# Attention and gated feed-forward in one kernel: softmax row sums turned and spread by VectorE, maxima over partitions by one transpose, and a new order of the steps

## The chip, the cores and the metric

The kernel runs on one core of one Trainium2 chip. The metric is the device time of one execution in microseconds. Three executions of the kernel before took 829.94, 830.16 and 830.75 us, a median of 830.16 us. The profiled execution, from which every row below is taken, took 830.94 us, and the span from its first to its last instruction is 829.1 us.

## The reference

Eight batches, twelve heads, 448 positions, head width 64. Attention with normalised queries and keys comes first; its output, heads side by side, is the input of a feed-forward layer with a three-tap convolution along the sequence as a gate.

```python
def _attn_ref(q, k, v, g_q, g_k):
    def rmsnorm(x, g):
        rms = np.sqrt(np.mean(x * x, axis=-1, keepdims=True) + 1e-06)
        return x / rms * g
    q_n, k_n = (rmsnorm(q, g_q), rmsnorm(k, g_k))
    scores = scale * np.matmul(q_n, k_n.transpose(0, 1, 3, 2))
    scores = scores - np.max(scores, axis=-1, keepdims=True)
    attn = np.exp(scores)
    attn = attn / (np.sum(attn, axis=-1, keepdims=True) + 1e-09)
    return np.matmul(attn, v)

def _moe_ref(x, w_in, conv_w, w_out):            # x: [8, 448, 768]
    h = np.maximum(x @ w_in, 0.0)                # w_in: [768, 1024]
    for k in range(3):                           # hp: h padded by one row at both ends
        conv_out += conv_w[k][None, None, :] * hp[:, k:k + S, :]
    gate = 1.0 / (1.0 + np.exp(-conv_out))
    return h * gate @ w_out                      # w_out: [1024, 768]
```

## The kernel before

Two heads of one batch make a pair; there are 48 pairs, n = 0 to 47, six to a batch. A pair's 2 x 448 query rows are laid end to end and cut into seven slots of 128. For a slot, TensorE makes the scores (`scores`, L643), VectorE takes their maximum (`soft_max`, L649), ScalarE makes the exponentials and, in the same instruction, their row sum (`soft_exp`, L657), which goes to one column of the tile `rsum` [128, 7]. The exponentials must stand with the keys on the partitions for the product with v. For pairs 0 to 9 TensorE turns them in f32 (`p_transpose`, L687). From pair 10 on, in six or five of the seven slots, they are split into two f16 parts (`p_hi`, `p_lo`) and turned by a DMA transpose on SP's queue (`p_turn`, L679).

The row sums are needed as divisors of the product with v, where the queries run along the free axis and 64 partitions of each head need the same row. So each pair does this: 1e-9 is added (`sum_add`, L710), VectorE takes the reciprocal (`sum_step`, L713), TensorE turns [128, 7] to [7, 128] in PSUM (`sum_transpose`, L716), ScalarE or VectorE copies that to `rT` (`sum_evac`, L99), a DMA stores it in DRAM as `rd` (`sum_store`, L724), and two DMAs read it back, each spreading one head's 448 numbers over 64 partitions of `rB` (`sum_load`, L730, 112 KB each). `x_scale` (L776, L779) multiplies the finished product with v by `rB` on VectorE, and so frees the product's PSUM bank; `x_hi` and `x_lo` split the result into two f16 parts.

A batch's six pairs are the contraction of the first feed-forward product (`in_part`, L849); its PSUM banks go through `in_relu`, `in_conv`, `in_tanh`, `in_gate`, `in_hi` and `in_lo`, and the second product (`out_part`, L918) makes the output, which is copied out by `out_evac` and stored by `out_store` (L932).

The two weight matrices and each batch's v are scaled by a power of two, from the largest absolute value. The maximum over partitions is taken in four steps: a column [128, 1] is turned to a row (`max_turn`, L191), VectorE reduces the row (`max_row`, L194), TensorE multiplies it by ones to spread it over the partitions again (`max_spread`, L199), and VectorE copies it (`all_max`, L204). That is done ten times, for two weights and eight batches.

What sets the order: each step is planned with a due time (`at`, from the tables `PACE` and `SHIFT`), its needs (`needs`), and its cost on each engine that may do it (`options`). A list scheduler then places step after step on the engine where it comes first, weighing readiness against urgency with the numbers in `PH`. It fixes the order on every engine, which engine takes a step that several may take, and the PSUM bank. Every engine then runs its list strictly in that order, and SP's list is the order in which DMAs are issued.

```python
        t = max((end + lat["DMA" if dma else e] for end, lat in ready[step]), default=0.0)
        kind = ("p_" if i else "f_") + PATIENCE.get(step[0], "")
        waiting[e][step] = t + PH.get(kind, 0.0), c, dma
```

Of the kernel before, what the change touches and what calls it, by code (L numbers as in the profile page):

```python
# [19 lines left out]
PH = dict(  # L20
    sw=0.0, f_pl=0.0372, f_ql=0.301, f_lo=0.0904, f_rms=0.0813, f_sq=0.2875, T=17.3632,
    ti=41.2236, si=4.107, so=8.3066, hop=0.89068, beta=0.014927, wi0=-54.4573, wi1=123.1391,
    wo0=27.8337, wo1=190.2785, cw=120.3485, p_evac=0.8292, p_hi=0.745, p_lo=1.5677, p_rms=0.1994,
    p_v=0.1678, p_x=0.3218, p_g=2.1286, p_relu=18.7486, p_cv=1.0141, p_ev=1.0461, sp=0.053009,
    nbulk=4, p_rs=0.042, p_sq=10.2108, p_w=182.8497, v0=27.1115, nd=6, cs=5, ct=3, cm=9, ne=5,
    n2=0, n1=10, q1=10, nf=10, pvs=4, p_sa=5.3829, p_c0=0.4104, p_ca=1.3841, p_ss=3.937,
    p_qh=3.8564, p_ql=3.3133, p_ph=10.4483, p_pl=23.3405, f_ca=0.5582, f_cv=0.0137, f_ev=0.0025,
    f_evac=0.001, f_g=0.001, f_relu=0.0326, f_v=0.1218, f_w=0.0241,
)
PACE = [  # L30
    20.0962, 19.9026, 16.7987, 18.8982, 12.5992, 14.6433, 12.4646, 10.3051, 23.0432, 17.7085,
    25.8722, 15.4055,
]
SHIFT = dict(
    prepare=752.847, load_g=657.535, make_g=976.01, load_cw=330.398, make_cw=2.091, load=33.068,
    convert=493.531, bound=434.297, bound_max=997.493, bound_turn=110.974, bound_row=439.308,
    bound_spread=144.878, scale=264.777, in_factor=855.239, split=253.006, rest=-5.488,
    out_factor=6.856, load_k=514.422, load_q=-22.79, square=152.084, square_sum=53.339,
    rsqrt=129.836, apply_rms=371.449, qk_transpose=946.516, qk_hi=163.782, v_load=526.719,
    v_bound=-7.992, scores=165.021, soft_max=-3.98, soft_exp=71.301, p_transpose=1089.978,  # L40
    p_evac=1.021, sum_add=292.102, sum_step=3.621, sum_transpose=7.451, sum_evac=951.667,
    sum_store=442.223, sum_load=7.241, pv=277.343, x_scale=531.668, x_hi=50.036, x_lo=5.449,
    v_max=-28.59, v_turn=474.043, v_row=421.545, v_spread=561.379, v_scale=1063.291, qk_lo=-6.16,
    q_hi=-16.404, q_lo=231.56, q_turn=97.487, p_hi=281.925, p_lo=-4.849, p_turn=602.22,
    p_low=0.089, v_hi=46.398, v_lo=369.031, moe_scales=639.368, in_part=826.195, in_relu=654.815,
    in_conv=84.909, in_tanh=377.101, in_gate=187.899, in_hi=137.708, in_lo=1.949,
    in_carry=294.262, out_scales=266.089, out_part=548.912, out_evac=315.656, out_store=-0.364,
# [23 lines left out]
def tile_attention_moe(ctx: ExitStack, tc, q, k, v, g_q, g_k, w_in, conv_w, w_out, out):  # L71
# [41 lines left out]
    def move(e, dst, src):  # L113
# [15 lines left out]
        rB=2, x32=1, vacc=2, vsc=4, cwb=3, rd=2, rsum=2, rT=2, mx=10, ph=4, vp=2,  # L129
# [3 lines left out]
    def new(tag, key, shape, dtype, pool=None):  # L133
        ring = rings.setdefault(tag, Ring(BUFS[tag]))
        pool = pool or sb
        t = pool.tile(
            shape, dtype, tag=tag, name=f"{tag}_{key}".replace(" ", "").replace(",", "_").strip("()"),
            bufs=BUFS[tag],
        )
        return ring.put((tag, key), t)  # L140

# [22 lines left out]
    ones = const.tile([1, P], F32, name="ones")  # L164
    phbuf = [const.tile([P, 2, 4, P], F16, name=f"ph{i}") for i in range(BUFS["ph"])]
    cw_in = const.tile([P, 3, NFC], conv_w.dtype, name="cw_in")
    cw = cw_in if conv_w.dtype == F32 else const.tile([P, 3, NFC], F32, name="cw")
# [4 lines left out]
    NGR = 13  # L172
    gring = const.tile([P, NGR, 2, S], F16, name="gring")
# [1439 lines left out]
```

## Time and profile before

| | before |
|---|---|
| median of 3 runs | 830.16 us |
| profiled execution | 830.94 us |
| its span, first to last instruction | 829.1 us |
| TensorE (PE) busy | 795.0 us, 96% |
| VectorE (DVE) busy | 688.6 us, 83% |
| ScalarE (ACT) busy | 687.6 us, 83% |
| GpSimd (POOL) busy | 451.1 us, 54% |
| DMA queue of SP, share of 16 engines | 75.9% |
| granted TensorE clock, mean | 0.996 |

Busy times are unions over an engine's instructions; instructions that overlap count once. TensorE's matmuls are pipelined and their ends modelled, so what a matmul costs is read from the distance between the starts of neighbours, not from its own duration. Of VectorE's instructions each overlaps the one before it by up to a tenth of a microsecond, so sums of single durations lie above the busy time. Since each engine runs its list in order, an instruction that waits holds all behind it on that engine.

### The profile page before, as it was taken

The page shows a single profiled execution, that of the slowest core. Times are in us where ns is not written, and L with a number is a line of the kernel's source. Part 1 is how long each engine was busy: PE and PEld are TensorE (multiplying, and loading weights), DVE is VectorE, ACT ScalarE, POOL GpSimd, SP SyncE. Part 2 cuts the span into 40 slices and gives each one's busy share as a digit, 9 for nine tenths or more (in the row PEclk, how much of TensorE's full clock was granted, in tenths as well). Part 3 has the DMA queues.
Part 4 walks back from the last instruction along what each step waited for, and adds up shares of the span by engine and source line. Part 5 has one row for each costly group of instructions (what it writes and reads, how often), then busy time and mean ns, then how long its engine had stood idle before and what let it go on. Part 6 is the DMA issues. An engine that isn't in the chain of part 4 may idle for free.

```text
span 829.1 us, 17139 instructions
## 1 busy us (share of the span) xinstructions
PE 795.0 (96%) x5650; PEld 434.0 (52%) x5650; DVE 688.6 (83%) x1387; ACT 687.6 (83%) x1613; POOL 451.1 (54%) x569
## 2 busy tenths in 40 slices
PE   3888999999999999999999999999999999999998
PEld 2434555555544555555545555555545565555554
DVE  7989999998799977999799978998799978781430
ACT  4979999998799977998899987998889978892531
POOL 1312123375677756685587667595587666461210
PEclk9998999999999999999999999999999999999999
DMA  9894644179999999878999999879998997564001
GB/s 244 209 203 104 184 133 124 48 128 201 184 182 182 180 190 196 190 148 195 196 177 185 182 195 200 174 163 192 203 175 179 193 180 161 100 120 102 11 21 57
DMA packets 325640, 132.47 MB, mean 160 GB/s; under 512 B 265312, under 2 KB 321968, under 8 KB 325552
## 3 DMA queue, kind: packets, MB, share of 16 engines
q1 hardware_dynamic: 325552, 131.39, 75.9%
q8 instruction: 44, 0.72, 0.4%
q14 instruction: 44, 0.36, 0.2%
HBM read 56.65 MB, written 11.18 MB: 82 GB/s over the span
## 4 chain that ended last, share of the span: by engine, by line
PE 59%; DVE 13%; ACT 13%; DMA 7%; issue 5%; POOL 2%; SPq 1%; ACTq 0%; POOLq 0%; DVEq 0%
PE bank L918 25%; PE bank L849 11%; PE bank L643 8%; PE bank L765 8%; PE bank L687 5%; DMA PT<-ph 3%; ACT ph L99 2%; PE bank L457 2%; DMA rB<-rd 2%; POOL ph L111 1%; DVE st L397 1%; DMA qkf<-in_q_dram 1%; DVE PT L703 1%; ACT sq L386 1%; ACT bank L857 1%
## 5 line engine op out<-in xcount | busy, mean ns | idle before, releaser
L849 PE MATMUL bank<-x,wi 128*128 128x448 f16 x1152 | 231.3, 353 | 0.1
L918 PE MATMUL bank<-wo,gring 128*128 128x384 f16 (+1 forms) x1056 | 200.0, 327 | 0.0
L849 PEld LDWEIGHTS <-wi 128*128 128x128 f16 x1152 | 110.9, 98 | 100.6 <-issue 7.7
L643 PE MATMUL bank<-kT,qT 64*128 64x448 f16 (+3 forms) x1072 | 131.7, 391 | 3.2 <-DVE wo L230 1.5
L918 PEld LDWEIGHTS <-gring 128*128 128x128 f16 (+1 forms) x1056 | 101.7, 99 | 62.7 <-issue 11.0
L765 PE MATMUL bank<-PT,vp 112*64 112x448 f16 x912 | 93.5, 354 | 0.0
L765 PEld LDWEIGHTS <-vp 112*64 112x64 f16 x912 | 48.5, 110 | 42.5 <-issue 11.2
L397 DVE TENSOR_REDUCE st<-sq 112x16 f32<-112x1024 f32 (+1 forms) x50 | 58.2, 1166 | 5.9 <-ACT sq L386 5.9
L111 POOL TENSOR_TENSOR x<-x,x 128x448 f16<-128x448 f32 x35 | 40.6, 1160 | 37.2 <-ACT x L99 20.4
L643 PEld LDWEIGHTS <-qT 64*128 64x128 f16 (+1 forms) x912 | 32.7, 97 | 48.8 <-issue 29.4
L386 ACT ACTIVATE sq<-qkf 112x1024 f32<-112x1024 f32 (+1 forms) x50 | 50.9, 1019 | 5.4 <-DMA qkf<-in_q_dram 4.0
L111 POOL TENSOR_TENSOR sq<-qkf,st 112x512 f32<-112x512 f32 x43 | 45.4, 1065 | 16.5 <-issue 6.8
L457 PE MATMUL bank<-ident,sq 112*128 112x112 f32 x232 | 32.9, 268 | 16.5 <-DVE st L433 10.5
L776 DVE TENSOR_TENSOR x<-bank,rB 128x448 f32<-128x448 f32 x38 | 23.7, 624 | 29.9 <-PE bank L765 14.2
L918 PE MATMUL bank<-wo,wi 128*128 128x384 f16 (+1 forms) x192 | 46.9, 326 | 0.0
L111 POOL TENSOR_TENSOR qkf<-sq,qkf 112x512 f16<-112x512 f32 x34 | 40.7, 1201 | 6.6 <-DMA PT<-ph 2.4
L703 DVE TENSOR_TENSOR PT<-bank,PT 112x512 f16<-112x512 f32 x57 | 39.0, 684 | 2.7 <-ACT PT L99 2.0
L710 POOL TENSOR_SCALAR rsum<-rsum 128x7 f32<-128x7 f32 x43 | 13.5, 315 | 50.4 <-ACT qT L99 10.1
L857 ACT ACTIVATE bank<-bank 128x448 f32<-128x448 f32 x64 | 33.9, 530 | 7.5 <-PE bank L849 6.7
L457 PEld LDWEIGHTS bank<-ident,sq 112*128 112x128 f32 x232 | 25.5, 143 | 26.6 <-issue 15.5
L99 ACT COPY PT<-bank 112x512 f32<-112x512 f32 x64 | 36.7, 581 | 3.0 <-PE bank L687 2.9
L111 DVE TENSOR_TENSOR sq<-qkf,st 112x512 f32<-112x512 f32 x53 | 39.0, 762 | 0.1
(2232 smaller groups left out, 1973.0 us busy)
## 6 DMA issues: line engine op xcount, KB each, us to landing
qkf<-in_k_dram SPq DMA_DIRECT2D x48, 224.0 KB
v<-in_v_dram SPq DMA_DIRECT2D x48, 224.0 KB
rB<-rd SPq DMA_DIRECT2D x96, 112.0 KB
wo<-in_moe_w_in_dram SPq DMA_DIRECT2D x12, 512.0 KB
gring<-in_moe_w_out_dram SPq DMA_DIRECT2D x16, 384.0 KB
qkf<-in_q_dram SPq DMA_DIRECT2D x24, 224.0 KB
qkf<-in_q_dram SPq DMA_DIRECT2D x48, 112.0 KB
PT<-ph SPq DMA_TRANSPOSE x209
```

The costliest lines, as they stand in the source:

```text
L99: (nc.scalar.copy if e == "ACT" else elementwise(e).tensor_copy)(dst, src)
L111: elementwise(e).tensor_tensor(dst, a, b, op=op)
L386: nc.scalar.activation(sq, x, AF.Square)
L397: nc.vector.tensor_reduce(st, sq, axis=AX.X, op=ALU.add)
L457: nc.tensor.transpose(ps[:, t * PB : (t + 1) * PB], x[:, t], ident[:PB, :PB])
L643: nc.tensor.matmul(ps[u][o, :S], lhs, rhs, start=(i == 0), stop=(whole(m) or i == 2),)
L687: nc.tensor.transpose(ps[:PB, kt * P : (kt + 1) * P], e[:, kt * PB : (kt + 1) * PB], ident)
L703: nc.vector.tensor_tensor(turned(n, j, 1), held["t", ("p", n, j)][:PB].rearrange("p (k q) -> p k q", k=NB), turned(n, j, 0), op=ALU.subtract,)
L765: nc.tensor.matmul(ps[HALF[h], :S], lhs, rhs, start=(i == 0 and k == 0), stop=(i == pvs(n)[-1] and k == NB - 1),)
L849: nc.tensor.matmul(ps[:, :S], wi[:, wl, c, fc * P : (fc + 1) * P], old("x", b * NP + c)[:, xl], start=(i == 0), stop=(i == 3 * NP - 1),)
L857: nc.scalar.activation(ps, ps, AF.Relu, scale=2.0 ** -24)
L918: nc.tensor.matmul(ps[p0 : p0 + m, :NO2], g, wo[:, wl, fc, half * NO2 : (half + 1) * NO2], start=(i == 0), stop=(i == 3 * NFC - 1),)
```

## The change

The turn of the row sums no longer passes TensorE and PSUM. `rsum` becomes [128, 32], two constant tiles cleared once, of which seven columns are used; `sum_turn` transposes it on VectorE in blocks of 32 x 32. The result [128, 32] has in block b, row s, the 32 sums of positions 32b to 32b+31 of slot s; the store to DRAM puts the four blocks side by side, so `rd` is [32, 128] and its first seven rows are what they were. For pairs 0 to 9 the two loads stay as they are. From pair 10 on (`sh=10`, `sm=15`) one load brings each head's row of 448 twice, to partitions 0, 32, 64 and 96 of a single constant tile `row`, and `sum_spread` copies the first partition of each 32 to all 32 with a VectorE shuffle, into `rB`. The tile `row` has one buffer, so a load waits for the shuffle of the pair before; `rT` has one buffer instead of two.

The maximum over partitions is now one transpose of the column repeated 128 times, [128, 128], so that every partition receives the whole row, and one VectorE reduction from PSUM. The steps `bound_row`, `bound_spread`, `v_row` and `v_spread` and the tile `ones` are gone. The convolution weights lie in the spare end of `wi32`, so that their load (`load_cw`) comes after the last `rest` of the first weight. The numbers of the scheduler (`PH`, `PACE`, `SHIFT`, some costs) are others, and for the first nine pairs the allowances on readiness have values of their own. The number of slots turned by DMA is the same for every pair.

```diff
-    sw=0.0, f_pl=0.0372, f_ql=0.301, f_lo=0.0904, f_rms=0.0813, f_sq=0.2875, T=17.3632,
+    sh=10, sm=15, sw=0.0, f_pl=0.0375, f_ql=0.2981, f_lo=0.1439, f_rms=0.7618, f_sq=0.4266,
...
-        rB=2, x32=1, vacc=2, vsc=4, cwb=3, rd=2, rsum=2, rT=2, mx=10, ph=4, vp=2,
+        rB=2, x32=1, vacc=2, vsc=4, cwb=3, rd=2, rsum=2, rT=1, row=1, ph=4, vp=2,
...
-    ones = const.tile([1, P], F32, name="ones")
+    sums = [const.tile([P, 32], F32, name=f"rsum{i}") for i in range(BUFS["rsum"])]
+    rows = [const.tile([P, S], F32, name=f"row{i}") for i in range(BUFS["row"])]
...
+    end = wi32[:, DM // P, 2 * S :]
+    cw = end[:, : 3 * NFC].rearrange("p (k c) -> p k c", k=3)
...
     def max_turn(key, col):
         t = bank("t", ("x", key))
-        nc.tensor.transpose(t[:1, :P], col, ident)
-
-    def max_row(key):
-        nc.vector.tensor_reduce(
-            new("mx", key, [1, 1], F32), held["t", ("x", key)][:1, :P], AX.X, ALU.max
-        )
-
-    def max_spread(key):
-        nc.tensor.matmul(
-            held["t", ("x", key)][:, 256:257], ones, old("mx", key), start=True, stop=True
-        )
+        nc.tensor.transpose(t[:, :P], col.to_broadcast([P, P]), ident)
 
     def all_max(dst_pow, key):
-        nc.vector.tensor_copy(dst_pow, held["t", ("x", key)][:, 256:257])
+        nc.vector.tensor_reduce(dst_pow, held["t", ("x", key)][:, :P], AX.X, ALU.max)
...
     def sum_step(n):
-        nc.vector.reciprocal(old("rsum", n), old("rsum", n))
-
-    def sum_transpose(n):
-        nc.tensor.transpose(
-            bank("t", ("r", n))[:NS, :P], old("rsum", n), ident
-        )
-
-    def sum_evac(n):
-        copy(on["sum_evac", n], new("rT", n, [NS, P], F32), held["t", ("r", n)][:NS, :P])
+        x = old("rsum", n)[:, :NS]
+        nc.vector.reciprocal(x, x)
+
+    def sum_turn(n):
+
+        nc.vector.transpose(new("rT", n, [P, 32], F32), old("rsum", n))
 
     def sum_store(n):
-        queue("rd").dma_start(new("rd", n, [NS, P], F32, pD), old("rT", n))
+        d = new("rd", n, [32, P], F32, pD)
+        queue("rd").dma_start(d.rearrange("s (b i) -> b s i", b=4), old("rT", n))
...
     def sum_load(n, h):
+        d = old("rd", n)[:NS].rearrange("t p -> (t p)").rearrange("(h s) -> h s", h=2)
+        if shuffled(n):
+            r = fixed("row", n, rows).rearrange("(x p) s -> x p s", p=32)[:, 0]
+            queue("rb").dma_start(r, d.unsqueeze(1).to_broadcast([2, 2, S]))
+            return
         if h == 0:
             new("rB", n, [P, S], F32)
-        row = old("rd", n).rearrange("t p -> (t p)")[h * S : (h + 1) * S]
-        queue("rb").dma_start(
-            old("rB", n)[HALF[h]], row.unsqueeze(0).to_broadcast([64, S])
-        )
+        queue("rb").dma_start(old("rB", n)[HALF[h]], d[h : h + 1].to_broadcast([64, S]))
+
+    def sum_spread(n):
+        nc.vector.stream_shuffle(new("rB", n, [P, S], F32), old("row", n), [0] * 32)
...
+        elif name == "load_cw":
+            for c in range(NWI):
+                yield "rest", "in", c
```

How the order moves is shown at three places. In the names a number that follows the tile is the pair or the batch; the last number only tells one use of a buffer from the next.

TensorE, around the turn of pair 30's sums: `bank2` takes the second feed-forward product of an earlier batch (`wo32`, `gring`, `wi32` hold its operands). Before:

```order
L918 MATMUL bank2_68<-wo32_85,gring_86 128x384
L918 LDWEIGHTS gring_86
L918 MATMUL bank2_68<-wo32_85,gring_86 128x384
L716 MATMUL bank6_72<-ident_76,rsum_30_6280 7x128
L918 LDWEIGHTS gring_86
L918 MATMUL bank2_68<-wo32_85,gring_86 128x384
```

In the change no such row is left for any of the 48 pairs; of L199's rows (`max_spread`) none is left either, and TensorE's list is otherwise of the same kinds and counts. It changes between groups of scores or of products with v and other work 249 times, where it did so 244 times.

SP, from the store of pair 30's sums to their last load: `PT` tiles are the turned exponentials, `ph` their source, `qT` turned queries, `v` and `qkf` inputs of later pairs. Before:

```order
L724 DMA rd_30_6628<-rT_30_6592 7x128
L932 DMA out_0_dram<-c_('o'_3_2_1_6622 128x384
L499 DMA_TRANSPOSE qT_33_6645<-qkf_33_6082 128x8x112
L679 DMA_TRANSPOSE PT_31_6594<-ph1_79 128x8x128
L730 DMA rB_30_6680<-rd_30_6628 64x448
L537 DMA v_36_6683<-in_v_dram 112x2x256
L361 DMA qkf_36_6699<-in_k_dram 112x2x256
L679 DMA_TRANSPOSE PT_31_6594<-ph2_80 128x8x128
L730 DMA rB_30_6680<-rd_30_6628 64x448
```

and in the change:

```order
L712 DMA rd_30_6539<-rT_30_6490 4x32x32
L669 DMA_TRANSPOSE PT_31_6488<-ph1_78 128x8x128
L669 DMA_TRANSPOSE PT_30_6252<-ph3_80 128x8x128
L726 DMA row0_83<-rd_30_6539 4x1x448
L497 DMA_TRANSPOSE qT_33_6593<-qkf_33_6059 128x8x112
```

One small load stands where two large ones did, and the last of it is issued after two other DMAs instead of after six.

VectorE, from the turn of pair 24's sums (`rsum0`) to the shuffle of them (`rB_24`), in the change; this pair has the least work between the two of all pairs from 10 to 46 (pair 36 as little):

```order
L708 STREAM_TRANSPOSE rT_24_5156<-rsum0_81 128x32
L639 TENSOR_REDUCE sst_(25_3_5160<-bank7_73 128x1
L639 TENSOR_REDUCE sst_(25_4_5173<-bank5_71 128x1
L837 TENSOR_TENSOR vsc_3_3775<-vsc_3_3775,wsc_88 128x1
L840 COPY vsc_2_2323<-vsc_3_3775 64x1
L841 COPY vsc_2_2323<-vsc_2_2323 64x1
L210 TENSOR_REDUCE vsc_4_5039<-bank2_68 128x1
L214 TENSOR_SCALAR vsc_4_5039<-vsc_4_5039 128x1
L217 TENSOR_SCALAR vsc_4_5039<-vsc_4_5039 128x1
L218 TENSOR_SCALAR vsc_4_5039<-vsc_4_5039 128x1
L395 TENSOR_REDUCE st_28_5090<-sq_29_5202 112x16
L639 TENSOR_REDUCE sst_(25_5_5232<-bank1_67 128x1
```

The row behind these is `L733 STREAM_SHUFFLE rB_24_5240<-row0_83 128x448`. Before, neither instruction was in VectorE's list, which went from the reciprocal to `x_scale` with no other step of the sums between, but for the seven pairs whose `rT` it copied.

## Rows read from the trace of the kernel before

**Rows 1.** Page, busy time (share of the span) by engine, with numbers of instructions.

```profile
PE 795.0 (96%) x5650; PEld 434.0 (52%) x5650; DVE 688.6 (83%) x1387; ACT 687.6 (83%) x1613; POOL 451.1 (54%) x569
```

**Rows 2.** Windows: stretch, length, each engine's busy us (instructions), clock, DMA share, GB/s.

```profile
core 0: us, PE busy (x) PEld busy (x) DVE busy (x) ACT busy (x) POOL busy (x), PEclk, DMA share, GB/s
0.00:156.00 156.00, 132.03 (x758) 71.89 (x759) 145.91 (x345) 137.16 (x333) 39.68 (x75) 0.98 0.64 163
156.00:728.00 572.00, 565.34 (x4229) 307.09 (x4228) 508.79 (x985) 506.55 (x1189) 388.13 (x470) 1.00 0.89 176
728.00:829.10 101.10, 97.61 (x666) 54.99 (x664) 33.95 (x59) 43.89 (x93) 23.28 (x25) 1.00 0.26 62
...
416.00:468.00 52.00, 50.98 (x410) 26.67 (x409) 51.19 (x92) 50.71 (x118) 39.91 (x46) 1.00 0.95 183
520.00:572.00 52.00, 51.74 (x372) 28.66 (x371) 49.80 (x96) 48.30 (x113) 35.67 (x47) 1.00 0.82 170
624.00:676.00 52.00, 51.37 (x438) 28.32 (x437) 49.10 (x92) 47.83 (x114) 38.58 (x45) 1.00 0.93 184
```

**Rows 3.** Timeline of PE around one L716: start, duration, instruction.

```profile
505.32 0.73 PE L849 MATMUL bank<-x,wi 128*128 128x448 f16 x3
505.89 0.27 PE L716 MATMUL bank<-ident,rsum 128*7 128x128 f32 x1
506.00 0.33 PE L918 MATMUL bank<-wo,gring 128*128 128x384 f16 x1
```

**Rows 4.** Timeline of PE around one batch's L199.

```profile
306.57 0.49 PE L918 MATMUL bank<-wo,wi 128*128 128x384 f16 x2
306.89 0.33 PE L918 MATMUL bank<-wo 128*128 128x384 f16 x1
307.15 0.38 PE L199 MATMUL bank<-mx,ones 1*128 1x1 f32 x2
307.46 1.31 PE L643 MATMUL bank<-kT,qT 64*128 64x448 f16 x12
```

**Rows 5.** Groups by line and form: busy, mean ns, idle before, releaser.

```profile
L716 PE MATMUL bank<-ident,rsum 128*7 128x128 f32 x48 | 13.2, 275 | 0.1
L99 ACT COPY rT<-bank 7x128 f32<-7x128 f32 x41 | 10.1, 247 | 1.8 <-PE bank L716 1.5
L99 DVE COPY rT<-bank 7x128 f32<-7x128 f32 x7 | 1.9, 269 | 0.0
L713 DVE RECIPROCAL rsum<-rsum 128x7 f32<-128x7 f32 x48 | 9.3, 194 | 3.9 <-POOL rsum L710 3.6
L418 DVE SCALAR_TENSOR_TENSOR st<-st 112x32 f32<-112x32 f32 x43 | 10.0, 232 | 0.3
L99 DVE CAST x<-x 128x448 f16<-128x448 f32 x8 | 3.8, 479 | 0.1
L776 DVE TENSOR_TENSOR x<-bank,rB 128x448 f32<-128x448 f32 x38 | 23.7, 624 | 29.9 <-PE bank L765 14.2 <-DMA rB<-rd 13.3 <-PE bank L918 1.2
L397 DVE TENSOR_REDUCE st<-sq 112x16 f32<-112x1024 f32 x46 | 55.5, 1208 | 3.0 <-ACT sq L386 3.0
L105 DVE TENSOR_SCALAR kT<-bank,G 128x448 f16<-128x448 f32 x22 | 14.8, 674 | 0.0
L99 DVE CAST PT<-bank 112x512 f16<-112x512 f32 x14 | 9.5, 681 | 1.1 <-PE bank L687 1.1
L194 DVE TENSOR_REDUCE mx<-bank 1x1 f32<-1x128 f32 x8 | 2.2, 276 | 4.4 <-PE bank L191 4.4
```

**Rows 6.** Page, DMA queue (packets, MB, share), and issues (count, KB each).

```profile
q1 hardware_dynamic: 325552, 131.39, 75.9%
...
rB<-rd SPq DMA_DIRECT2D x96, 112.0 KB
```

**Rows 7.** Timeline of SP, one pair's store to its second load.

```profile
480.26 0.64 SPq L724 DMA_DIRECT2D rd<-rT  x1
...
482.87 0.54 SPq L730 DMA_DIRECT2D rB<-rd  x1
...
486.46 0.58 SPq L730 DMA_DIRECT2D rB<-rd  x1
```

**Rows 8.** Timeline of DVE: one L649 row and the `x_scale` of that pair.

```profile
488.56 0.61 DVE L649 TENSOR_REDUCE sst_(31_4_6565<-bank 128x1 f32<-128x448 f32 x1
489.81 0.64 DVE L776 TENSOR_TENSOR x<-bank,rB 128x448 f32<-128x448 f32 x1 [0.64 <-issue]
```

**Rows 9.** Chain that ended last, 400 to 420 us: start, duration, what.

```profile
411.25 4.07 DMA rB<-rd
```

**Rows 10.** Waits: engine, line, releaser: us in total, times, longest us.

```profile
DVE x L776 <- DMA rB<-rd: 13.3, 13, 2.0
ACT ph L99 <- DMA PT<-ph: 19.8, 23, 2.3
```

More of the change, by code (lines that the diff above doesn't have):

```diff
@@ L37 @@
[L37 to L42, printed above, removed]
@@ new lines @@
+    load=31.489, convert=814.375, bound=1163.815, bound_max=1185.545, bound_turn=683.508,
+    scale=1588.906, in_factor=1190.579, split=219.334, rest=-3.777, out_factor=13.562,
+    load_k=276.969, load_q=-23.205, square=644.465, square_sum=176.751, rsqrt=204.636,
+    apply_rms=466.723, qk_transpose=49.891, qk_hi=700.581, v_load=1413.524, v_bound=41.813,
+    scores=154.339, soft_max=-4.033, soft_exp=1280.605, p_transpose=1204.209, p_evac=1.285,
+    sum_add=984.669, sum_step=662.828, sum_store=217.691, sum_load=507.067, pv=524.491,
@@ L654, in soft_exp @@
         if j == 0:
-            new("rsum", n, [P, NS], F32)
+            fixed("rsum", n, sums)
         c = slot(n, j)
@@ L809, in plan_attention @@
         at(s + 2.5, sum_step, n)
-        at(s + 3.0, sum_transpose, n)
-        at(s + 3.5, sum_evac, n)
+        at(s + 3.0, sum_turn, n)
         at(s + 4.0, sum_store, n)
-        for h in range(2):
+        for h in range(loads(n)):
             at(s + 6.0, sum_load, n, h)
+        if shuffled(n):
+            at(s + 7.0, sum_spread, n)
         if nd(n):
@@ L1190, in needs @@
             yield "sum_store", n
-            yield "x_scale", n - BUFS["rB"]
+            if shuffled(n):
+                for m in range(n):
+                    yield "sum_spread", m
+            else:
+                yield "x_scale", n - BUFS["rB"]
             if a[1]:
                 yield "sum_load", n, 0
+        elif name == "sum_spread":
+            yield "sum_load", n, 0
+            yield "x_scale", n - BUFS["rB"]
         elif name == "pv":
@@ L1207, in needs @@
             yield "x_lo", n - BUFS["x32"]
-            for h in range(2):
-                yield "sum_load", n, h
+            if shuffled(n):
+                yield "sum_spread", n
+            else:
+                for h in range(2):
+                    yield "sum_load", n, h
         elif name == "x_hi":
@@ L1392, in tile_attention_moe, with patience @@
     waiting = {e: {} for e in ("PE", "DVE", "ACT", "POOL", "SP")}
+    MOE = ("in_", "out_", "moe_")
+    def patience(i, name, *a):
+        kind = ("p_" if i else "f_") + PATIENCE.get(name, "")
+        if a and isinstance(a[0], int) and a[0] < (1 if name.startswith(MOE) else PH["early"]):
+            kind += "_early"
+        return kind
     def enqueue(step):
@@ L1396, in enqueue @@
             t = max((end + lat["DMA" if dma else e] for end, lat in ready[step]), default=0.0)
[L1397 to L1398 removed]
+            waiting[e][step] = t + PH.get(patience(i, *step), 0.0), c, dma
     sys.setrecursionlimit(20000)
@@ L1472, in tile_attention_moe @@
             enqueue(step)
-    SCHED.update(most=most, nd=nd, steps=steps, options=options, needs=needs, takes=takes, give=give, BUFS=BUFS, PATIENCE=PATIENCE,
+    SCHED.update(most=most, nd=nd, steps=steps, options=options, needs=needs, takes=takes, give=give, BUFS=BUFS, PATIENCE=PATIENCE, patience=patience,
                  LAT=LAT, OVER=OVER, ISSUE=ISSUE, shared=shared, BULK=BULK, mode=mode)
```

134 lines of the change are left out of this document (63 added, 71 removed).

## The prediction

> **What bounds the kernel now.** I read the page first, then windows over three stages, then timelines of single instructions. The page says that TensorE is busy 96% of the span, VectorE and ScalarE 83% each [rows 1]. A share over the whole span hides its stages, so the windows come next [rows 2]. In the first 156 us TensorE is busy 132.0 us, so it idles 24 us; VectorE is busy 145.9 of the 156. There TensorE waits for VectorE and ScalarE: the f32 pairs run, and the weights are converted. From 156 to 728 us TensorE is busy 565.3 of 572 us, at a granted clock of 1.00, and idles only 6.7 us. This is the stage that bounds the kernel, and its bound is TensorE's list. In the last 101 us the feed-forward products of the last batches remain, TensorE is busy 97.6 us, and VectorE has little to do. In the middle stage VectorE is busy 508.8 of 572 us and the DMA engines have a share of 0.89, so both stand close behind.
>
> Two things follow. A matmul that is taken out of the middle stage shortens it by the distance between the starts of its neighbours, if the others keep up. And no wait that is cured there can give more than 6.7 us in all.
>
> **The turn of the sums on TensorE goes.** In the timeline a turn of `rsum` starts at 505.89 and the next matmul at 506.00, while the three L849 ahead of it run at their usual distance (505.32 to 505.89) [rows 3]. So a turn takes 0.11 us of TensorE's list. Its own duration of 275 ns [rows 5] is the depth of the pipeline and would overstate it two and a half times. 48 x 0.11 = 5.3 us.
>
> **The spreading of the maxima goes.** The pair of L199 instructions stands from 307.15 to 307.46, 0.31 us [rows 4]; ten of them make 3.1 us. The transpose ahead of them stays and still streams 128 columns; that it now fills 128 output partitions instead of one is counted as nothing, with 10 x 0.11 = 1.1 us as the upper bound if it took twice as long.
>
> Together 8.4 us. Ten of the turns and four of the maxima (both weights, batches 0 and 1) lie in the first stage, 10 x 0.11 + 4 x 0.31 = 2.3 us. TensorE idles there, so only half of it is counted: 7.2 us remain. If all or none of the 2.3 counts, it is 8.4 or 6.1.
>
> **Changes of kind.** In front of L199 the last L918 takes 0.26 us to the next start, where the two before it take 0.16 [rows 4]. TensorE's list has five more changes between scores, products with v and the rest; at 0.10 us each that is 0.5 us more.
>
> **VectorE gets more.** A turn of 128 x 32 is not in this trace. From below it is bounded by the reciprocal of seven columns, 194 ns, from above by 232 ns for a two-input operation on 32 columns [rows 5]; with 0.21, 48 make 10.1 us. A shuffle of 128 x 448 is not in it either. The cheapest row over 448 columns is the cast at 479 ns, the dearest comparable the copy of 512 columns at 681 ns; nearest in columns, type and output is `x_scale`, 624 ns [rows 5]. 38 x 0.62 = 23.7 us, between 18.2 and 25.9. The Trainium skill (VectorE: DVE Perf Modes, The perf-mode tier table) gives the shuffle a price, about 2400 ns for 2048 elements in its one mode; scaled to 448 that is an estimate of 525 ns, and the 38 would be 19.9 us, while the sum of the forecast, where they are covered, stays the same. What VectorE loses: seven copies of `rT` (7 x 0.269 = 1.9), ten reductions of a row (10 x 0.276 = 2.8), and 18 of its 23 evacuations of `kT` go to ScalarE (18 x 0.674 = 12.1); it takes over 13 evacuations of `PT` (13 x 0.681 = 8.9) [rows 5]. Net about +26 us; smaller moves are not priced. Some 23 of them fall in the middle stage, where VectorE would be busy 532 of 572 us, 93%. I cost this at nothing, because TensorE sets the pace and VectorE has 63 us of idle time there [rows 2]. If that cover goes, it costs up to the whole 23.
>
> **ScalarE** loses 41 copies of `rT` (10.1 us [rows 5]) and gains the `kT` evacuations; nothing counted.
>
> **DMA.** 76 of 96 loads of 112 KB go, 8.7 of 131.39 MB [rows 6], or 6.6%; 38 loads of 7 KB and a wider store come. By bytes that would be 0.066 x 0.759 x 829 = 42 us of the engines' time at most. What waits for it now: VectorE 13.3 us at `x_scale` and ScalarE 19.8 us for a free `ph` [rows 10], both behind TensorE's pace. Between 0 and the 6.7 us of TensorE's idle time; I take 0, since the same wait appears again at the shuffle.
>
> **The wait at the shuffle.** VectorE's list is in order, so the shuffle holds all scores' maxima behind it until its row has landed. Before, a store was issued at 480.26, its first load at 482.87, its second at 486.46 [rows 7], and `x_scale` started at 489.81 [rows 8], at most 3.4 us behind the issue; elsewhere the chain has 4.1 us [rows 9]. With one load, issued 2.6 us behind the store, a row lands 6.0 to 6.7 us after the store's issue. In the new order the work between turn and shuffle is least at pair 24: three maxima at 0.61 [rows 8], one reduction at 1.21 [rows 5], one of 0.28 and six small ones of some 0.2, about 4.5 us; VectorE then waits some 2 us. The other pairs have mostly 6 to 9 us by the same pricing. If a dozen pairs wait 1.5 us each, that is 18 us in place of the 13.3 now: VectorE's own idle time, and nothing more is counted.
>
> **The sum.** 830.94 - 7.2 + 0.5 = 824.2 us, against the profiled execution. That one is 0.78 us above the median, so against the median I expect **823.5 us**.
>
> **Rivals.**
> 1. *The first stage gets better too.* It has 24 us of TensorE idle time, and its steps get their own numbers in the scheduler. Against it: VectorE is busy 94% there and receives ten turns more. If a third of the idle time went, 8 us, the time would be 815.5.
> 2. *Nothing is won, since VectorE is the next bound.* In the three fullest windows it is busy 51.2, 49.8 and 49.1 of 52 us [rows 2], and 23 us over 572 add 2.1 to each 52: the first is over-full, the other two full. If TensorE waits 2 us in each of these three, 6 us, 829.5 remain. For it speak these windows; against it, that they can pass work to ScalarE, which has fewer evacuations of sums.
> 3. *Slower: the row comes late at every shuffle.* Place: pairs 10 to 47, the shuffle at the head of VectorE's list, the maxima of the next scores behind it, TensorE behind those. The store now writes 128 pieces of 128 bytes (the tile is [128, 32]) where it wrote seven of 512. The point that decides is a row that takes longer than the 7 us of a typical cover. At 2 us beyond it, 38 x 2 = 76 us of waits would fill the 63 - 23 = 40 us that VectorE has left, and up to 36 would reach TensorE; ScalarE and the order's slack take a part of these, and with half of them the time is 823.5 + 18 = 841; at 1 us beyond, 38 us would just fit. The Trainium skill (DMA: Bandwidth & Descriptors, Specifications) speaks for this rival: it asks for at least 512 bytes a piece and has smaller ones written by read-modify-write. No row of this trace shows the time of such a store by itself; by that rule the store would be slower, and by the 2.6 us of the rows it would not matter.
> 4. *The change does not do what it says* can be left out: in the new order the turns, the loads and the spreading matmuls are gone from the lists.
>
> **How the numbers follow.** About 0.2%, 1.7 us, is what a measurement of this kernel can tell from no change: 828.5 to 831.8. I give the forecast 0.52; its own range is 819 to 828.5, with the 6.1 and 8.4 us of the first two terms, a few microseconds for the idle time that the DMA relief may give, and the same for waits at the shuffle. Rival 1 has 0.21, rival 2 0.13, rival 3 0.14. Faster is the forecast and rival 1, 0.73; same is rival 2, 0.13; slower is rival 3, 0.14. The range runs from 815, which leaves out a part of rival 1, to 832, which leaves out nearly all of rival 3.
>
> **What would show it.** No turn of `rsum` on TensorE; in 156 to 728 us a stretch of the same work shorter by some 6 us at nearly full busy time. The turn at about 0.21 us, the shuffle at about 0.62, VectorE at some 93% of the middle stage. At the shuffle waits of some 20 us in total with row loads as releaser; over 60 us, with TensorE's idle time in the middle stage above 15 us, would mean rival 3. TensorE idle time in the first 156 us well under 24 us means rival 1. The prediction is wrong if TensorE's idle time in the middle grows by the 6 us that its list lost, or if the time falls without that list being the reason.

## The result and the profile after

The changed kernel takes **819.88 us** (median of four executions, 819.17 to 821.95) where the kernel before took 830.45 (four, 829.94 to 831.14). The ratio is 0.9876, with a 95% interval of 0.9857 to 0.9896: 10.3 us faster. The forecast of 823.5 us was 3.6 us too high; the time lies in its range, near its fast end of 819, and the gain is above the 8.4 us that the two terms of its sum allow at most. The profiled execution took 819.89 us, its span is 818.1 us.

The page of the changed kernel, busy time by engine, and the three stages of the windows view (stretch, length, busy us with instructions of PE, PEld, DVE, ACT, POOL, clock, DMA share, GB/s):

```profile
PE 787.5 (96%) x5582; PEld 429.3 (52%) x5582; DVE 704.5 (86%) x1478; ACT 683.4 (84%) x1584; POOL 445.9 (55%) x575
```

```profile
0.00:156.00 156.00, 134.16 (x769) 73.07 (x770) 146.24 (x346) 138.93 (x333) 46.96 (x88) 0.98 0.61 167
156.00:728.00 572.00, 566.85 (x4239) 307.11 (x4237) 530.17 (x1080) 511.97 (x1190) 382.23 (x471) 1.00 0.87 164
728.00:818.10 90.10, 86.47 (x578) 49.10 (x576) 28.14 (x55) 32.54 (x64) 16.72 (x17) 1.00 0.20 53
```

Against [rows 1, 2], TensorE is 7.5 us less busy in total and as full as before in the middle stage: 5.2 us idle of 572, where it was 6.7. VectorE is 21.4 us fuller there, as the turns and shuffles were bound to make it. The groups of the new operations, by form, then the shuffle's and ScalarE's waits:

```profile
L733 DVE STREAM_SHUFFLE rB<-row 128x448 f32<-128x448 f32 x38 | 24.9, 656 | 0.0
L708 DVE STREAM_TRANSPOSE rT<-rsum 128x32 f32<-128x32 f32 x48 | 9.7, 202 | 0.2
L109 DVE CAST PT<-bank 112x512 f16<-112x512 f32 x25 | 17.0, 680 | 0.0
L115 DVE TENSOR_SCALAR kT<-bank,G 128x448 f16<-128x448 f32 x5 | 3.4, 672 | 0.0
```

```profile
DVE rB L733 <- DMA row<-rd: 11.2, 16, 1.6
ACT ph L109 <- DMA PT<-ph: 26.4, 34, 2.6
```

The shuffle waits for its row 16 times, 11.2 us in all, in place of the 13.3 us of `x_scale` before [rows 10]. ScalarE's wait for a free `ph` did not shrink with the large loads, it went from 19.8 to 26.4 us.

Where the time came from is read from the second feed-forward product, whose first instruction closes the first stage. The source view of L918, before and then after (count, duration min/median/max in ns, first and last start in us):

```profile
L918 PE MATMUL bank<-wo,gring x1056: 323/326/350, 177.7 to 824.8; 128*128 128x384 f16 x155, 128*64 128x384 f16 x21
```

```profile
L918 PE MATMUL bank<-wo,gring x1056: 322/326/350, 173.1 to 813.7; 128*128 128x384 f16 x153, 128*64 128x384 f16 x23
```

It starts 4.6 us earlier (177.7 to 173.1) and ends 11.1 us earlier. So some 4.6 us come from ahead of this product, where the forecast had counted 1.2 (half of 2.3), and 6.5 from behind its start, where it had counted 5.5 (7.2 - 1.2 - 0.5).

### The profile page after: what moved, and what is told of

Read it like the earlier page. It is cut to its first block, busy times and chain, and to the rows that moved or that the text cites. A ratio compares the mean times of both kernels' runs of the same rounds, so it can differ in the third digit from the quotient of the medians.

```text
span 818.1 us, 16993 instructions
## 1 busy us (share of the span) xinstructions
PE 787.5 (96%) x5582; PEld 429.3 (52%) x5582; DVE 704.5 (86%) x1478; ACT 683.4 (84%) x1584; POOL 445.9 (55%) x575
## 3 DMA queue, kind: packets, MB, share of 16 engines
q1 hardware_dynamic: 325364, 123.56, 74.4%
## 4 chain that ended last, share of the span: by engine, by line
PE 48%; DVE 13%; ACT 11%; DMA 6%; issue 4%; POOL 2%; SPq 2%; ACTq 0%; POOLq 0%; DVEq 0%
PE bank L918 21%; PE bank L849 11%; PE bank L764 6%; PE bank L633 6%; DMA PT<-ph 4%; PE bank L677 2%; ACT ph L109 2%; SPq L669 1%; PE bank L455 1%; POOL ph L121 1%; DMA rd<-rT 1%; DVE st L395 1%; DMA row<-rd 1%; DVE PT L693 1%; ACT bank L857 1%
## 5 line engine op out<-in xcount | busy, mean ns | idle before, releaser
L918 PE MATMUL bank<-wo,gring 128*128 128x384 f16 (+1 forms) x1056 | 199.5, 327 | 1.0 <-ACT e_(34_4_7306 L647 0.8
L918 PEld LDWEIGHTS <-gring 128*128 128x128 f16 (+1 forms) x1056 | 101.7, 99 | 67.9 <-issue 16.4
L764 PEld LDWEIGHTS <-vp 112*64 112x64 f16 x912 | 50.5, 110 | 42.1 <-issue 15.0
L121 POOL TENSOR_TENSOR sq<-qkf,st 112x512 f32<-112x512 f32 x38 | 39.9, 1056 | 19.1 <-issue 9.6
L121 POOL TENSOR_TENSOR x<-x,x 128x448 f16<-128x448 f32 x33 | 34.2, 1036 | 27.6 <-DVE x L109 12.3
L455 PE MATMUL bank<-ident,sq 112*128 112x112 f32 x232 | 33.0, 268 | 15.8 <-DVE G L974 10.3
L918 PE MATMUL bank<-wo,wi 128*128 128x384 f16 (+1 forms) x192 | 46.9, 326 | 0.0
L121 DVE TENSOR_TENSOR sq<-qkf,st 112x512 f32<-112x512 f32 x58 | 44.8, 791 | 0.1
L121 POOL TENSOR_TENSOR qkf<-sq,qkf 112x512 f16<-112x512 f32 x32 | 37.1, 1160 | 5.6 <-DVE sq L121 4.1
L918 PE MATMUL bank<-wo,carry 128*64 128x384 f16 x192 | 34.0, 328 | 0.5 <-DVE c_(1_6_3169 L879 0.5
L542 DVE TENSOR_REDUCE vacc<-v 112x1 f32<-112x512 f32 x48 | 32.2, 674 | 2.4 <-DMA v<-in_v_dram 1.9
```

The source lines that it names most:

```text
L121: elementwise(e).tensor_tensor(dst, a, b, op=op)
L455: nc.tensor.transpose(ps[:, t * PB : (t + 1) * PB], x[:, t], ident[:PB, :PB])
L542: nc.vector.tensor_reduce(old("vacc", b)[:PB, i : i + 1], old("v", n).rearrange("p h t d -> p (h t d)"), axis=AX.X, op=ALU.max, apply_abso ...
L764: nc.tensor.matmul(ps[HALF[h], :S], lhs, rhs, start=(i == 0 and k == 0), stop=(i == pvs(n)[-1] and k == NB - 1),)
L918: nc.tensor.matmul(ps[p0 : p0 + m, :NO2], g, wo[:, wl, fc, half * NO2 : (half + 1) * NO2], start=(i == 0), stop=(i == 3 * NFC - 1),)
```

## The experiments

Four theories were set against one another. **P**: TensorE's list sets the pace of the middle stage, and each instruction taken off it is won. **O**: the gain comes from the new order. **V**: VectorE sets the pace. **D**: the large loads held up the DMAs. In microseconds below, a ratio is multiplied by 830.45; against the changed kernel means less its 0.9876.

### One part of the change at a time, in the order of before

*The maxima alone.* The reduced row then stands in all partitions, and the spreading matmul is left out:

```diff
-        nc.tensor.transpose(t[:1, :P], col, ident)
+        nc.tensor.transpose(t[:, :P], col.to_broadcast([P, P]), ident)
...
-        nc.vector.tensor_copy(dst_pow, held["t", ("x", key)][:, 256:257])
+        nc.vector.tensor_copy(dst_pow, old("mx", key))
```

> The kernel before with its own order; only the maxima are taken in the new way (one transpose of the repeated column, one reduction; the spreading step issues nothing). Theory P (TensorE's list sets the pace of the middle stage): the 20 spreading matmuls go, 10 x 0.31 us = 3.1 us, of which those of the first 156 us count half: 1.9 to 3.1 us faster than before, 827.3 to 828.6. Theory O (the gain comes from the new order and not from the work taken off TensorE): within 1 us of before. Theory V (VectorE sets the pace): no change, as VectorE keeps its three steps.

Measured: 0.9987 (0.9971 to 1.0004), 1.1 us faster and not clear of nothing.

*The turn alone.* The sums are turned by VectorE at the place of the old turn, the large loads stay:

```diff
-        nc.tensor.transpose(
-            bank("t", ("r", n))[:NS, :P], old("rsum", n), ident
-        )
+        nc.vector.transpose(new("rT", n, [P, 32], F32), old("rsum", n))
...
+        queue("rd").dma_start(d.rearrange("s (b i) -> b s i", b=4), old("rT", n))
```

> The kernel before with its own order; only the row sums are turned by VectorE, at the place where TensorE turned them, and the copy from PSUM is gone; the two large loads stay for all pairs. Theory P: 48 x 0.11 us leave TensorE's list, 38 of them in the middle stage: 4.2 to 5.3 us faster than before, about 825.5. Theory O: within 1.5 us of before. Theory V: slower by some of the 8 us that VectorE gains (48 x 0.21 less 7 x 0.27), 832 to 838.

Measured: 0.9993 (0.9981 to 1.0006). The 48 turns left TensorE's list, and the time did not move. In the middle stage:

```profile
156.00:728.00 572.00, 561.58 (x4185) 302.51 (x4184) 510.28 (x1011) 500.54 (x1155) 381.89 (x470) 1.00 0.92 177
```

TensorE idles 10.4 us where it idled 6.7. What was taken off its list came back as waiting. VectorE, at 510 us, is hardly fuller than before (509), which speaks against V. On SP the store takes longer, a median of 582 ns where it took 320:

```profile
L728 SPq DMA_DIRECT2D rd<-rT x48: 563/582/897, 33.1 to 753.4; - x48
```

*Turn, small load and shuffle together*, the shuffle right ahead of `x_scale`:

```diff
+        if n >= 10:
+            nc.vector.stream_shuffle(old("rB", n), old("rB", n), [0] * 32)
```

> As the run with the turn alone, and from the eleventh pair on one small load in place of two large ones and a VectorE shuffle right ahead of x_scale, in place in the tile of the divisors. Still the order of before. Theory P: VectorE has room for 23.7 us more, so the time stays within 1.5 us of the run with the turn alone, about 825. Theory V: 5 to 20 us slower than the turn alone. If the large loads held the DMA engines up (theory D), 2 to 6 us faster than the turn alone.

Measured: 0.997 (0.9955 to 0.9985), 2.5 us faster; 1.9 us of that by the step from large loads to small ones, although VectorE carries the shuffles. By the intervals of both runs the step lies between 0.3 and 3.5 us.

*All three operations in the order of before.*

```diff
+        nc.tensor.transpose(t[:, :P], col.to_broadcast([P, P]), ident)
...
+        nc.vector.transpose(new("rT", n, [P, 32], F32), old("rsum", n))
...
+            nc.vector.stream_shuffle(old("rB", n), old("rB", n), [0] * 32)
```

> The order, the scheduler's numbers and the engines of the steps stay those of before; all three changes of operations are made in it (maxima by one repeated turn, sums turned by VectorE, one small load and an in-place shuffle right ahead of x_scale from pair 10 on). Singly the maxima gave a ratio of 0.9987 and turn plus shuffle 0.997. Theory A (the operations add up, and are worth some 3 to 4 us in a fixed order; the rest of the 11 us came with the new order): a ratio of 0.9957, 826.9 us, between 825.5 and 828.5, and the first second-stage product no earlier than before by more than 1 us. Theory O (the order is only a carrier; together the operations give most of the gain): 823 us or less. If the parts hinder each other: 828.5 or more.

Measured: 0.9974 (0.9959 to 0.9988), 2.2 us faster. That is no more than the parts would add up to (3.6 us; the difference is within the intervals), and far from 10.3. So in the old order the operations give about a fifth of the gain.

### The scheduler's numbers alone

The changed operations, planned with the numbers of before (`PH`, `PACE`, `SHIFT`), and the operations of before, planned with the new numbers and the separate allowances for the first pairs. A part of the first edit (the second is its reverse):

```diff
 PACE = [
-    19.5944, 19.8948, 16.4648, 19.6082, 13.2431, 14.9147, 11.825, 10.1937, 22.5592, 19.3385,
-    25.6034, 15.2494,
+    20.0962, 19.9026, 16.7987, 18.8982, 12.5992, 14.6433, 12.4646, 10.3051, 23.0432, 17.7085,
+    25.8722, 15.4055,
```

> The operations of the changed kernel, ordered with the scheduler's numbers of before (no values of their own for the first nine pairs). Theory P: the work taken off TensorE counts in any order that keeps it fed: 3 to 8 us faster than before, 822.5 to 827.5, with the first stage up to 156 us as before (the start of the second feed-forward product near 177 us). Theory O: within 2 us of before, or slower.

> The operations of before, ordered with the scheduler's numbers of the change (its due times, allowances, and values of their own for the first nine pairs). Theory P: the gain in the first stage, 4.5 us up to the start of the second feed-forward product, came from these numbers, and the rest of the order is worth nothing: 1 to 4 us faster than before, 826 to 829, with that start near 173 us. Theory O: most of the 10.6 us, 820 to 823.

Measured: 1.0081 (1.0053 to 1.0109) for the new operations with old numbers, 1.0213 (1.0184 to 1.0241) for the old operations with new ones. Both are slower than before, the second against every expectation. Neither half carries the gain, so theory O, taken alone, falls too. The numbers seem to fit only the operations that they were chosen with. The old ones have no shift of the due time for the two new steps, so the first plan is also an untuned one.

### One cost added or taken away, in the order of the change

*No shuffle.* Two large loads stand where the small load and the shuffle stood, 24.9 us of VectorE fewer; `rB` has a third buffer:

```diff
-            queue("rb").dma_start(r, d.unsqueeze(1).to_broadcast([2, 2, S]))
+            for i in range(2):
+                queue("rb").dma_start(old("rB", n)[HALF[i]], d[i : i + 1].to_broadcast([64, S]))
...
-        nc.vector.stream_shuffle(new("rB", n, [P, S], F32), old("row", n), [0] * 32)
```

> The changed kernel with its own order; in place of the one small load and the shuffle, two large loads at the place of the load, for all pairs, with one more buffer for the divisors. Theory P: the shuffle is covered and the large loads were covered, so within 1.5 us of the changed kernel, 818.5 to 821.5. Theory V: VectorE loses 23.7 us, so 3 to 10 us faster than the changed kernel. Theory D: 2 to 6 us slower, 822 to 826, with more waits of ScalarE for DMA transposes.

Measured: 1.0076 (1.0055 to 1.0096), 16.6 us above the changed kernel, where theory D had expected 2 to 6. Middle stage, and ScalarE's wait:

```profile
156.00:728.00 572.00, 555.66 (x4125) 300.35 (x4123) 504.26 (x985) 498.63 (x1155) 375.98 (x462) 1.00 0.90 176
```

```profile
ACT ph L109 <- DMA PT<-ph: 37.3, 43, 2.7
```

VectorE is 26 us emptier there and TensorE idles 16.3 us instead of 5.2. The wait that grew is not one for `rB` but ScalarE's for the transposes of `ph`, DMAs that stand behind the loads in SP's list.

*48 more transposes on TensorE*, 128 x 7 to 7 x 128 like the old turn, into a part of a bank of the second feed-forward product that nobody reads:

```diff
+            nc.tensor.transpose(ps[:NS, NO2:], ident[:, :NS], ident)
```

> The changed kernel with its own order, and 48 extra f32 transposes on TensorE of the size of the old turn of the sums (7 columns of weights, 128 columns streamed), one ahead of each of the first 48 blocks of the second feed-forward product, into unused columns of its bank; nobody waits for them. Theory P: each costs its 0.11 us, 48 x 0.11 = 5.3 us, 825.1. Theory O or V: TensorE has idle time to hide them, under 2 us, below 822.

Measured: 0.9912 (0.9893 to 0.9932), 3.0 us above the changed kernel where their places on the list make 5.3. With both intervals that is 0.7 to 5.3 us, so in this order P holds for a part, perhaps for all.

*Each shuffle twice*, the second over the first:

```diff
+        for _ in range(2):
+            nc.vector.stream_shuffle(rb, old("row", n), [0] * 32)
```

> The changed kernel with its own order, each of the 38 shuffles done twice: 23.7 us more on VectorE. Theory P: VectorE would be busy some 554 of 572 us of the middle stage, so part of the cover is gone; 2 to 8 us slower, 822 to 828, well under the 23.7 us added. Theory V (VectorE already sets the pace): close to the full 23.7 us, 838 to 844.

Measured: 0.9996 (0.9979 to 1.0012), 10.0 us above the changed kernel for 24.9 us of added VectorE work, a little above what P had expected. VectorE's cover is partly used up; 0.4 us is lost for each microsecond added.

### Bytes or issues

To split theory D, two loads were added behind each row load, into a spare place in DRAM that nobody reads, once as large as the old ones and once as small as the row load:

```diff
+            for i in range(2):
+                queue("rb").dma_start(z[HALF[i]], d[i : i + 1].to_broadcast([64, S]))
```

```diff
+            for i in range(2):
+                queue("rb").dma_start(z[:, i], d.unsqueeze(1).to_broadcast([2, 2, S]))
```

> The changed kernel with its order, its small row load and its shuffle as they are; right behind each of the 38 row loads SP issues two more loads of 112 KB of the same source into a spare place in DRAM, which nobody reads. No engine waits for them, so the only thing that returns of the old loads is their share of the DMA engines and of SP's list. The version with two large loads in place of load and shuffle stood 16.5 us above the changed kernel. Theory D (the large loads hold up the transfers behind them, the turned exponentials above all): most of that returns, 830 to 837 us, with ScalarE's wait for the transposes of ph at 33 us or more (26.4 in the changed kernel, 37.3 with the large loads). Theory W (what cost there was x_scale waiting for a late row or the missing shuffle): 820 to 823 us and that wait near 26.

> As the run with spare large loads, but the two spare loads behind each row load are small, 7 KB each like the row load itself. The number of DMAs that SP issues is the same as there, the bytes are not. Theory D-bytes (the time that the packets take on the DMA engines is what holds up the others): no more than 2 us above the changed kernel, 819 to 822. Theory D-issue (each DMA on SP's list costs its place there, 76 of them 0.5 to 0.6 us each): half or more of what the large spare loads cost, 825 or more.

Measured: 1.0378 (1.0346 to 1.0409) with the large spare loads, 41.7 us above the changed kernel; 1.0231 (1.021 to 1.0252) with the small ones, 29.5 us above it. The first is far above the 830 to 837 us expected of theory D: the spare loads come on top of the row loads and the shuffles, which the run with two large loads did without. The larger loads' bytes are worth 12 us; the other 29.5 us come with 76 DMAs of 7 KB that nobody reads. The queue in the page, with the small ones (packets, MB, share of 16 engines), is no busier than the changed kernel's 74.4%, which speaks against the packets:

```profile
q1 hardware_dynamic: 325820, 124.10, 71.2%
```

Of theory D the greater part stands in the form of D-issue, beside the 12 us that go with the bytes. ScalarE's wait for `ph` in the run with small spare loads:

```profile
ACT ph L109 <- DMA PT<-ph: 53.5, 57, 2.6
```

*The store with fewer pieces.* The 25 unused rows of each block of 32 are not stored; that takes four stores of seven pieces:

```diff
-        queue("rd").dma_start(d.rearrange("s (b i) -> b s i", b=4), old("rT", n))
+        for b in range(4):
+            x = old("rT", n)[32 * b : 32 * b + NS]
+            queue("rd").dma_start(d[:NS, 32 * b : 32 * b + 32], x)
```

> The changed kernel, but the store of the turned sums leaves out the 25 unused rows of each block of 32: four stores of 7 pieces of 128 bytes instead of one of 128 such pieces. The 25 rows of rd that nobody reads are not written; the output is the same. If the many small pieces make the row late (rival 3 in small): VectorE waits at the shuffle fall from 11.2 to 6 us or less and the time by 1 to 3 us, 817 to 819. If a store's time does not hang on its pieces, three more DMAs a pair on SP's list only cost: 820 to 823 us, the waits at the shuffle at 11 us or above.

Measured: 1.0137 (1.0113 to 1.016), 21.7 us above the changed kernel, where 0 to 3 had been expected for the three further stores. Waits at the shuffle rose from 11.2 to 33.0 us:

```profile
DVE rB L735 <- DMA row<-rd: 33.0, 30, 2.8
```

So this run says nothing on the time that small pieces take to land. It agrees with a price of a DMA on SP's list, but does not separate that from the later row.

### What SP's list costs

What a DMA takes on SP is a row of the trace. The source views of the store and of the two kinds of load (count, ns min/median/max, first and last start), before:

```profile
L724 SPq DMA_DIRECT2D rd<-rT x48: 282/320/861, 34.6 to 754.1; - x48
L730 SPq DMA_DIRECT2D rB<-rd x96: 450/538/1514, 37.8 to 757.5; - x96
```

after:

```profile
L712 SPq DMA_DIRECT2D rd<-rT x48: 541/574/646, 31.7 to 739.4; - x48
L726 SPq DMA_DIRECT2D row<-rd x38: 532/542/614, 186.6 to 741.5; - x38
L730 SPq DMA_DIRECT2D rB<-rd x20: 450/470/1180, 37.0 to 168.5; - x20
```

and the added or changed ones of the runs with large loads back, with small spare loads, with large spare loads and with four stores:

```profile
L727 SPq DMA_DIRECT2D rB<-rd x76: 457/579/1413, 187.8 to 759.5; - x76
```

```profile
L729 SPq DMA_DIRECT2D spare<-rd x76: 554/564/1060, 189.8 to 774.9; - x76
```

```profile
L729 SPq DMA_DIRECT2D spare<-rd x76: 518/577/1497, 188.5 to 786.8; - x76
```

```profile
L714 SPq DMA_DIRECT2D rd<-rT x192: 269/293/914, 32.2 to 765.8; - x192
```

A load of 7 KB keeps SP as long as one of 112 KB, 0.54 us by both medians. The large loads back are 76 x 0.579 - 38 x 0.542 = 23.4 us more on SP, for 16.6 us of time. The small spare loads are 76 x 0.564 = 42.9, for 29.5. The four stores are 192 x 0.293 - 48 x 0.574 = 28.7, for 21.7. That is 0.71, 0.69 and 0.76 us of time for each microsecond of SP's list. The agreement is weaker than it looks. The first run also carries the larger loads' bytes (some 12 us by the two spare runs) and is rid of the shuffles (some 10 us by the doubled shuffle), two terms that nearly cancel; the third also makes rows late at the shuffle. Only the small spare loads come near to adding nothing else. The large spare loads, 43.9 us of SP and 41.7 of time, stand higher, which fits bytes that come on top.

SP's timeline in the changed kernel at a full place (start, duration, line):

```profile
464.29 0.52 SPq L359 DMA_DIRECT2D qkf<-in_k_dram  x1
464.86 0.46 SPq L535 DMA_DIRECT2D v<-in_v_dram  x1
465.43 2.63 SPq L669 DMA_TRANSPOSE PT<-ph  x2
468.11 0.58 SPq L369 DMA_DIRECT2D qkf<-in_q_dram  x1
468.73 0.57 SPq L712 DMA_DIRECT2D rd<-rT  x1
469.40 2.61 SPq L669 DMA_TRANSPOSE PT<-ph  x2
472.11 0.61 SPq L726 DMA_DIRECT2D row<-rd  x1
472.78 0.40 SPq L932 DMA_DIRECT2D out_dram<-c_('o'_3_0_0_6073  x1
473.28 2.66 SPq L669 DMA_TRANSPOSE PT<-ph  x1
475.98 0.57 SPq L932 DMA_DIRECT2D out_dram<-c_('o'_3_0_1_6150  x1
```

Each issue starts within 0.12 us of the end of the one before. A DMA more in such a stretch moves every transpose of exponentials behind it. Not every stretch is like this one. Added up over the middle stage, SP's DMA instructions take some 446 of 572 us (458 before), and in between SP itself waits, longest for GpSimd's part of `ph`:

```profile
SPq L669 <- POOL ph L121: 56.6, 42, 7.9
```

So SP's list is not full. What an added DMA costs there, as far as the waits show, is that the transposes behind it start later.

The Trainium skill (DMA: Bandwidth & Descriptors, Issuing engines are not separate DMA queues) says that the time a sequencer needs to start a DMA is usually small relative to the DMA itself. For one large load the trace agrees: 0.54 us on SP, and 4.07 us of such a load on the chain [rows 7, 9]. But in this kernel 365 plain DMAs and 247 transposes share one list, and the runs above show that DMAs added to it cost time. What no run separates is SP's own time from anything that the queue behind it does per DMA.

## Why the prediction was right, and which steps of it were not

**The bound.** The forecast's account of TensorE came true. Its busy time fell by 7.5 us, both times at a mean granted clock of 0.996, where the sum had 8.4 - 0.5 = 7.9 for the whole list. Its idle time in the span fell by 3.5 us (34.1 to 30.6), 2.1 of them in the first 156 us, and the middle stage is as full as before (566.9 of 572). That a shorter list is enough is not confirmed. With the same operations in the old order 2.2 us were won, and with the turn alone TensorE's idle time in the middle grew from 6.7 to 10.4 us, toward the sign that the forecast had named for being wrong. The condition "if the others keep up" was assumed and not worked out; it held in the new order and, with the turn alone, not in the old one. In that the forecast had luck: nothing in its sum tells the one order from the other.

The bound was read from 6.7 us of idle time, but an engine with little idle time can still be held by others a little everywhere: in the new order 48 transposes put back cost 3.0 of 5.3 us, a second shuffle 10.0 of 24.9, and added DMAs some 0.7 of each microsecond on SP.

**The turn of the sums, 5.3 us.** By itself, in the old order, it gave 0.6 (between a gain of 1.6 and a loss of 0.5). The step that failed is "a matmul that is taken out of the middle stage shortens it by the distance between the starts of its neighbours, if the others keep up". They did not keep up there. One thing that grew is the store: that of 128 pieces keeps SP 0.582 us in this run where that of seven kept it 0.320, 48 x 0.262 = 12.6 us more on SP's list. The forecast had priced the wider store by when it lands (rival 3) and not by what it takes to issue. That this is what ate the gain is not shown, as no run has the turn without the wider store, and at 0.7 us for each microsecond it would have been 8.8 us, more than the 5.3.

**The maxima, 3.1 us.** By themselves 1.1, with an interval from a gain of 2.4 to none. That the repeated column adds nothing to the transpose is right by its row: L207 at 392.88 is followed by the next matmul at 392.99, 0.11 us.

```profile
392.88 0.27 PE L207 MATMUL bank<-ident,vsc 128*128 128x128 f32 x1
392.99 1.46 PE L918 MATMUL bank<-wo,gring 128*128 128x384 f16 x8
```

**VectorE.** The turn took 202 ns (forecast 210), the shuffle 656 (forecast 620). The Trainium skill (VectorE: DVE Perf Modes, The perf-mode tier table) gives about 2400 ns for 2048 elements; the forecast's estimate of 525 ns from it is not borne out by the 656. The middle stage is at 530.2 us busy, forecast 532. All of VectorE gained 15.9 us and not 26. Of the priced moves, the casts of `PT` went from 14 to 25 and those of `kT` from 22 to 5, about as forecast [rows 5]; the rest of the difference lies in moves that were not priced. The cost of nothing is doubtful: by the doubled shuffle, 24.9 us of further shuffles cost some 10 us in this order. Whether the first ones cost as much, inside the result, no run shows.

**DMA, costed at nothing: the step with the weakest ground.** It was bounded by TensorE's idle time in the middle, 6.7 us, and "I take 0, since the same wait appears again at the shuffle". The bound on a gain held: that idle time fell by 1.5 us. But putting the loads back costs 16.6 us, since idle time can grow by more than it can shrink. The wait that grew with it is not at the shuffle or at `x_scale` but ScalarE's for the DMA transposes. The issues of 0.54 to 0.64 us stood in [rows 7] and were read for when a row lands, not for what they hold up. SP's list had for these DMAs 48 x 0.320 + 96 x 0.538 = 67.0 us before, and has 48 x 0.574 + 38 x 0.542 + 20 x 0.470 = 57.5 now: 9.5 us shorter. At 0.7 us each that would be 6.6 us, about what came behind the first L918. This is only a sum that fits, as TensorE's own account does. Two things speak against a fixed price. ScalarE's wait for `ph`, in which the added DMAs show, is longer in the changed kernel than before (26.4 and 19.8 us). And in the old order the same wait fell from 25.4 us with the turn alone to 13.4 with the small loads, for 1.9 us of time:

```profile
ACT ph L99 <- DMA PT<-ph: 25.4, 27, 2.6
```

```profile
ACT ph L99 <- DMA PT<-ph: 13.4, 17, 2.0
```

**The wait at the shuffle.** 11.2 us in 16 waits, the forecast had 18 in a dozen. Pair 24, whose cover was priced at 4.5 us with a wait of 2, had none; its shuffle started 7.0 us behind the turn, because VectorE had waited for TensorE's turn of a maximum (0.99 us) and for ScalarE's squares (1.85) on the way:

```profile
390.56 0.20 DVE L708 STREAM_TRANSPOSE rT<-rsum 128x32 f32<-128x32 f32 x1
...
393.19 0.29 DVE L210 TENSOR_REDUCE vsc<-bank 128x1 f32<-128x128 f32 x1 [0.99 <-PE bank L207]
...
395.89 1.22 DVE L395 TENSOR_REDUCE st<-sq 112x16 f32<-112x1024 f32 x1 [1.85 <-ACT sq L384]
...
397.57 0.65 DVE L733 STREAM_SHUFFLE rB<-row 128x448 f32<-128x448 f32 x1
```

**Rival 1, the first stage.** It came true by about a half at most: 4.6 us by the first L918, where the rival had 8. Its own sign is weak, as TensorE's idle time in the first 156 us fell from 24.0 to 21.8 us; the forecast's 2.3 us of shorter list, counted whole, would be the other half. It belongs to the order. Of the runs that were traced, those in the order of the change that leave the first pairs as they are start L918 earlier than 177.7 too, the one with two large loads at 174.3:

```profile
L919 PE MATMUL bank<-wo,gring x1056: 323/326/351, 174.3 to 830.1; 128*128 128x384 f16 x153, 128*64 128x384 f16 x23
```

In the order of before, with the new operations, it starts within 1.1 us of 177.7 in all four runs, and in the two plans with numbers and operations crossed it starts later, at 185.2 and 182.5. Which of the new places in the first stage does it was not tried.

**Rival 2** (VectorE next bound) has its mechanism, by the doubled shuffle, but not its size. **Rival 3** (the row late at every shuffle) did not come. The run with four stores has 33.0 us of waits there and is slower than before, though its longer list on SP is in that too.

What stays open: why the order of before can't turn the shorter list of SP into time, and what in the two plans decides it. Taking costs away in the old order gave a fifth of the gain; adding one to the new order cost 0.4 to 0.8 of it. No run was faster than the changed kernel.

## What to carry to other kernels

Count the issuing queue as an engine: add up what each DMA takes on it (count x median of its rows) and look in its timeline for gaps, before judging DMAs by bytes; a load of 7 KB took as long to issue as one of 112 KB. A store that is cut into more pieces costs at the issue too, so put its issue time beside what the other engine saves. In this kernel, whose order is fitted to its operations, one operation at a time in the old order gave far less than the change as a whole; and what an added cost loses in one order is not what its removal wins in another.

## What had not been expected of the hardware

A DMA of seven pieces of 512 bytes kept SP 0.320 us (median of 48), seven pieces of 128 bytes 0.293 (of 192), 128 pieces of 128 bytes 0.574 (of 48), four rows of 1,792 bytes 0.542 (of 38), 64 such rows 0.538 (of 96). The issue time follows neither the bytes nor the pieces alone. And 38 pairs of loads that nobody reads made the program 29.5 us longer, 0.39 us a load, while ScalarE's wait for DMA transposes on the same queue grew from 26.4 to 53.5 us.
